# Fused attention and mixture of experts: whole weights eight blocks ahead, conversion beside the first expert, one scatter a block, the end in halves

## The chip, the cores and the metric

The kernel runs on one core of a Trainium2 chip. The metric is device time in microseconds (us) of one execution; three runs of the kernel before gave 1216.66, 1218.28 and 1219.01 us. PE is the matmul engine, DVE, ACT and POOL are the vector, scalar and GpSimd engines, and SP issues the plain DMAs. POOL issues the indirect ones (gathers and scatters by row number).

## The reference

Everything is float32. Three stages follow one another (cut to what is computed):

```python
# 1 attention, 4 batches x 12 heads, 448 tokens, 64 wide
q_n, k_n = rmsnorm(q, g_q), rmsnorm(k, g_k)
attn_out = softmax(q_n @ k_n.T / 8) @ v            # -> x: 1792 tokens x 768
# 2 mixture of experts, 8 experts, each takes exactly 224 tokens
logits = x @ w_gate                                # 1792 x 8
for idx in argsort(-logits.flatten()):             # greedy by rank
    tok, e = idx // 8, idx % 8
    if assigned[tok] < 0 and counts[e] < 224:
        assigned[tok] = e; counts[e] += 1
out[mask_e] = relu(x[mask_e] @ w1[e]) @ w2[e]      # 768 -> 1024 -> 768
# 3 one dense layer over all tokens
h = x @ w_in; g = h * sigmoid(1.702 * h); y = g @ w_out   # 768 -> 2048 -> 768
```

`w_in` and `w_out` are given in 64 bit and are converted to float32 by the kernel itself.

## The kernel before, in words

**Attention** fills the first 330 us: heads are software pipelined in an order written out by hand, and the token rows `x` are written to DRAM (`xd`) pair of heads by pair of heads: `xtok` (transposes into PSUM), `put_x` (scaling by 1/sum on DVE, L305, and a store). For the last three pairs `put_x(pr, True)` copies the PSUM tile on ACT (L301) and scales it on POOL.

**Routing** ranks the tokens for one expert at a time (phase k gives the tokens of expert slot k): `choose`, `row` (PE transposes), compares of every token against every other (`compare`, DVE, L569, L571, and L575 for the diagonal piece `Bd`), rank matmuls (L592, L598), `close` (which expert is full first, a one-hot tile `O` at L643, matmuls at L650, and the row numbers `idx`). Phase 0 (`first`) is done beside the end of attention. After phases 1 and 3 `together` packs the tokens that remain: 16 and 12 scatters on POOL (L695, 112 rows of 40 bytes each, one column `j` of tokens a scatter), then one load of the packed rows `rec` on SP.

**Moe.run** goes through four groups `pr`: expert 2pr, expert 2pr+1, then the dense layer on the 448 tokens of both. An expert is 8 blocks with a tile of `w1` and 6 with a tile of `w2`; the dense part has 16 blocks with a tile of `w_in` (18 matmuls of 448 columns) and 12 with half a tile of `w_out` (24 matmuls). Below, n counts the blocks of an expert or a dense part. Experts 0 and 1 (`FULL`) use the float32 weights as loaded, with 6 or 8 matmuls a block; all others split weights and activations into a high and a low fp32r part (`whi` on ACT, `wlo` on POOL or DVE) and need three matmuls for one. Weights are loaded by `load` into `raw` (4 buffers), at most `LOAD` = 4 blocks ahead of the one in use, in `ahead`.

**Between blocks** `back(budget)` spends a credit: it issues routing steps, each with a cost written in its `yield`, and conversion steps as long as `conv.steps < due`, where `due` grows by `rate` a block. A negative cost ends the routing of that block. As long as phase 1 isn't done only routing is issued. Where a phase is needed at once `until(k)` issues all of its steps: before expert 0, at block 13 of expert 0, at block 5 of experts 2, 4, 6 (for the next expert) and at dense block 20 (for the next pair).

**Conversion** (`Convert`) has 48 pieces of 512 KB: a load, two copies on ACT (`words`, L887 and L888), then two steps, one DVE instruction each (L901, L906), and a 256 KB store. 43 of the 96 steps are issued during attention; `load` of a dense block calls `until(need)` so that its words exist.

**The end**: the last dense block (d = 5) sums 48 matmuls into one tile of 448 columns; then come one copy on ACT (L1115), four transposes (L1120), one copy on DVE (L1125) and four scatters on POOL (L1137).

Of the kernel before, what the change touches and what calls it, by code (L numbers as in the profile page):

```python
# [20 lines left out]
FT = mybir.dt.float32  # L21
# [30 lines left out]
class Attn:  # L52
# [240 lines left out]
            nc.tensor.transpose(p[:, i], s.xuT[pr][:, i * 112:(i + 1) * 112], s.ident128)  # L293
        s.px = p

    def put_x(s, pr, end=False):
        nc, p = s.nc, s.px
        b, pl = divmod(pr, 6)
        if end:
            xt = s.io.tile([112, 4, 256], FT, name="kt", bufs=3)[:, 0:2].rearrange("p a (b c) -> p (a b) c", c=128)  # L300
            nc.scalar.copy(xt, p)  # L301
            p = xt
        else:
            xt = s.wk.tile([112, 4, 128], FT, name="xt", bufs=2)
        (nc.gpsimd if end else nc.vector).tensor_tensor(xt.rearrange("p i (h d) -> p i h d", d=64), p.rearrange("p i (h d) -> p i h d", d=64),  # L305
                                s.rinv[b][:, :, 2 * pl:2 * pl + 2, None].to_broadcast([112, 4, 2, 64]), op=OP.mult)
        nc.sync.dma_start(s.xd[b * 448:(b + 1) * 448, pl * 128:(pl + 1) * 128].rearrange("(i p) d -> p i d", p=112),
                          xt)
# [63 lines left out]
    def run(s, slot, beside):  # L372
# [87 lines left out]
        beside(BESIDE[0])  # L460
        s.gate_b(s.B - 1, 1)
        beside(0)
        for pr in (last - 2, last - 1, last):
            s.xtok(pr, True)
            s.put_x(pr, True)
        beside(BESIDE[1])


class Route:
# [4 lines left out]
    def __init__(s, tc, pool, wk, rec, identf, out_ids, dram):  # L474
# [2 lines left out]
        s.wk, s.rec, s.identf = wk, rec, identf  # L477
        s.L = rec[:, :, 0:8]
        s.done = [None] * 8
        s.pend, s.group, s.moving = [], {}, False  # L480
        ii = wk.tile([112, 224], I32, name="ii", bufs=1)
        s.before = pool.tile([112, 112], FT, name="before")
        nc.gpsimd.iota(ii[:, 0:112], pattern=[[1, 112]], base=0, channel_multiplier=-1)
# [186 lines left out]
    def together(s, n, n2, small):  # L670

        nc, V, wk = s.nc, s.nc.vector, s.wk
        al = s.alive[:, 0:n]
        f = [wk.tile([112, 16], FT, name="f%d" % i)[:, 0:n] for i in range(2)]
        src, sh, i = al, 1, 0
        while sh < n:
            V.tensor_copy(f[i][:, 0:sh], src[:, 0:sh])
            V.tensor_tensor(f[i][:, sh:], src[:, sh:], src[:, 0:n - sh], op=OP.add)
            src, i, sh = f[i], 1 - i, 2 * sh
        V.tensor_tensor(f[i], src, al, op=OP.subtract)  # L680
        yield -1.5
        q = small()[0:112, 0, 0:n]
        nc.tensor.matmul(q, s.before, al, start=True, stop=False)
        nc.tensor.matmul(q, s.ones, f[i], start=False, stop=True)
        yield -0.1
        pos = wk.tile([112, 16], I32, name="pos")[:, 0:n]
        V.tensor_tensor(f[0], q, s.own[:, 0:n], op=OP.subtract)
        V.tensor_tensor(f[0], f[0], al, op=OP.mult)
        V.tensor_tensor(pos, f[0], s.own[:, 0:n], op=OP.add)
        yield -0.5  # L690
        sc = []
        s.moving = True
        for j in range(n):
            nc.gpsimd.memset(s.spacer, 0.0)
            st = nc.gpsimd.indirect_dma_start(  # L695
                out=s.left[n2][:, :], out_offset=bass.IndirectOffsetOnAxis(ap=pos[:, j:j + 1], axis=0),
                in_=s.rec[:, j, :], in_offset=None)
            for x in sc:
                s.tc.declare_no_dep(st.ins, x.ins, reason="rows of other tokens")
            sc.append(st)  # L700
            if j % 2:
                yield -0.05
        s.moving = False
        rec = wk.tile([112, 16, 10], FT, name="rec", bufs=1)[:, 0:n2]
        nc.sync.dma_start(rec, s.left[n2][0:112 * n2, :].rearrange("(p j) c -> p j c", j=n2))
        yield -0.1
        V.tensor_copy(s.ids[:, 0:n2], rec[:, :, 8:10])
        V.memset(s.alive, 1.0)
        s.rec, s.L = rec, rec[:, :, 0:8]
        yield 0.4  # L710
# [33 lines left out]
    def first(s, rank, wide, small, buffer, buffer2):  # L744
# [60 lines left out]
        for j in range(12, 16):  # L805
            compare(j, 12, 16)
        s.flush()
        cnt = wide()
        s.counts(0, 12, cnt)
        nc.scalar.copy(s.ct[:, 12:16], bank[3])  # L810
# [110 lines left out]
class Moe:  # L921
# [15 lines left out]
        s.nl = s.nsp = s.used = 0  # L937
        s.raw, s.hl, s.reg, s.late = {}, {}, {}, {}

    LOAD, SPLIT, LOOK = 4, 2, 5  # L940

    def load(s, n):
        kind, e, i = s.chunks[n]
        if kind in ("w1", "w2") and e not in s.reg:
            s.reg[e] = s.nc.sync.value_load(s.r.eid[0:1, e:e + 1], min_val=0, max_val=7)
        K = 6 if kind == "w1" or (kind == "w32" and i < 16) else 8
        t = s.pw.tile([128, 8, 128], FT, name="raw", bufs=4)[:, 0:K]
        if kind == "w32":
            s.conv.until(s.need(n))
            if i < 16:  # L950
# [33 lines left out]

    def ahead(s):
        N = len(s.chunks)
        while s.nl < N and s.nl < s.used + s.LOAD - (s.used > 0 and s.whole(s.used - 1)):
            kind, e, _ = s.chunks[s.nl]
            if kind != "w32" and not s.r.done[e]:
                break  # L990
            if s.nl >= s.nsp + 4:
                break
            s.load(s.nl)
            s.nl += 1
        while s.nsp < s.nl and s.nsp < s.used + s.SPLIT:
            s.split(s.nsp)
            s.nsp += 1
# [91 lines left out]
    def pair(s, pr, zs):  # L1089
# [12 lines left out]
        s.low()  # L1102
        pend = None
        for d in range(6):
            p = s.ps.tile([128, 448], FT, name="mm", bufs=3)
            for h in range(2):
                w = s.weights()
                for f in range(8):
                    ff = 8 * h + f
                    s.mm3(p, w, f, (gs[:, ff, 0], gs[:, ff, 1]), ff == 0, ff == 15)  # L1110
                if h == 0 and pend:
                    pend()
                yield
            oT = s.pa.tile([128, 448], FT, name="sg", bufs=3)
            nc.scalar.copy(oT, p)  # L1115

            def pend(oT=oT, d=d):
                q = s.ps.tile([112, 4, 128], FT, name="tr", bufs=2)
                for t in range(4):
                    nc.tensor.transpose(q[:, t], oT[:, t * 112:(t + 1) * 112], s.ident128)  # L1120

                def put():
                    if d % 3 == 0:
                        s.ot = s.pa.tile([112, 4, 384], FT, name="ot", bufs=1)
                    nc.vector.tensor_copy(s.ot[:, :, d % 3 * 128:(d % 3 + 1) * 128], q)  # L1125
                    if d % 3 == 2:
                        s.sc += [(pr, s.ot, d // 3, t) for t in range(4)]
                s.ev.append(put)
        s.last = pend

    def store(s, n):
# [30 lines left out]
    def back(s, budget, stay=False, idle=False):  # L1162
# [5 lines left out]
        while s.credit > 0:  # L1168
            if used > 0.5:
                s.low(False)  # L1170
            if not s.r.done[1]:
                c = abs(s.r.step())
            elif s.conv.gen and s.conv.steps < s.due + (0 if route else 2):
                c = s.conv.step()
                if c is None:
                    s.conv.gen = None
# [17 lines left out]
    def run(s):  # L1194
# [6 lines left out]
        s.ahead()  # L1201
        for _ in range(4):
            s.r.step()
        for d in (0, 2, 4):
            s.xsplit(0, d)
            s.r.step()
            s.low()
        for pr in range(4):
            zs = s.pa.tile([128, 6, 2, 448], FR, name="zs", bufs=1)
            for e in (2 * pr, 2 * pr + 1):  # L1210
                early, done = None, 0
                for n, _ in enumerate(s.expert(e, zs)):
# [11 lines left out]
                    if e == 0 and s.r.done[1]:  # L1224
# [3 lines left out]
                        elif n > early + 1 and done < 6:  # L1228
                            s.xsplit(1, done)
                            done += 2  # L1230
                    s.back(0 if n == 7 else (3.1 if e == 0 else 1.4 if e == 1 else 0.6 if n < 8 else 1.2), True if e > 1 and n % 2 == 1 else None, e in IDLE and (e % 2 == 1 or bool(s.r.done[e + 1])))
                if e == 0:
                    s.ahead()
                    for d in range(done, 6, 2):
                        s.xsplit(1, d)
                    s.rate = 0.7
                elif e == 1:
                    s.rate = 1.9
            for n, _ in enumerate(s.pair(pr, zs)):
# [13 lines left out]
def kernel(  # L1253
# [31 lines left out]
    with ExitStack() as actx:  # L1285
# [18 lines left out]

        attn.run(slot, beside)
        for _ in early:
            pass

    rps = ctx.enter_context(tc.tile_pool(name="r_ps", bufs=1, space=bass.MemoryType.PSUM))
    route.start(rps, ctx.enter_context(tc.tile_pool(name="r_wk2", bufs=2)), 1)  # L1310
# [32 lines left out]
```

## Time and profile before

| | |
|---|---|
| runs | 1216.66, 1218.28, 1219.01 us (median 1218.28) |
| the profiled execution's own time | 1219.52 us |
| its span, first to last instruction | 1217.7 us |
| mean granted clock of PE | 0.968 of full |
| busy share of the span | PE 94%, DVE 59%, POOL 53%, ACT 51% |
| data moved | 172.98 MB, mean 142 GB/s |

The profiled execution lies 1.24 us above the median of the runs. The windows further down name a stage by its time: expert 0 375.57 to 425.94, expert 1 to 477.88, the dense part of the first pair to 549.48 (`w_in`) and 616.23 (`w_out`), expert 2 to 653.55, expert 3 to 686.27, and so on. In a view's row "x" is a count, "idle before <-" is the engine's idle time ahead of the instruction and what released it; "remote" is a release that the profile can't put to an instruction.

### The profile page before, as it was taken

To read this page: it belongs to the slowest core of one execution; us is meant where nothing else is said; L and a number is where in the kernel's file an instruction comes from. 1 tells how busy PE (TensorE), PEld (TensorE's weight loads), DVE (VectorE), ACT (ScalarE), POOL (GpSimd) and SP (SyncE) were. 2 spreads that over 40 slices of the span, in tenths; PEclk is the share of its full clock that TensorE was granted. 3 is DMA by queue.
4 is the path that set the end of the run, shared out by engine and by line. 5 is a ranking of instruction groups with operands and counts; after the bars stand their busy time and mean duration, and the time that the engine had idled before them with its cause. 6 is when DMAs were issued, how large, how long until landed. Compare 5 with 4: busy or idle time off the path is not lost.

```text
span 1217.7 us, 20040 instructions
## 1 busy us (share of the span) xinstructions
PE 1146.2 (94%) x7432; PEld 982.7 (81%) x7432; DVE 722.8 (59%) x1398; ACT 626.0 (51%) x1261; POOL 646.6 (53%) x570
## 2 busy tenths in 40 slices
PE   4899999999958979999999999999999999999995
PEld 3677666777536969788899988989998999999994
DVE  7699999999787416989654467454447203421100
ACT  4798889988632124765245544234544324445420
POOL 2688878884430232445555845536444565454552
PEclk9799999999967989999999999999999999999998
DMA  6445464533114657886567534338733345753421
GB/s 160 131 131 144 115 163 127 138 91 89 39 43 125 175 146 214 274 268 223 165 178 192 160 92 133 111 92 211 197 117 116 120 121 166 191 169 107 137 81 34
DMA packets 185505, 172.98 MB, mean 142 GB/s; under 512 B 9536, under 2 KB 159808, under 8 KB 185408
## 3 DMA queue, kind: packets, MB, share of 16 engines
q1 hardware_dynamic: 180080, 160.55, 46.1%
q0 software_dynamic: 4224, 11.14, 3.1%
q8 instruction: 58, 0.95, 0.3%
q14 instruction: 39, 0.32, 0.1%
q10 hardware_dynamic: 1104, 0.03, 0.0%
HBM read 147.96 MB, written 23.72 MB: 141 GB/s over the span
## 4 chain that ended last, share of the span: by engine, by line
PE 78%; DVE 13%; DMA 2%; ACT 2%; issue 2%; POOL 1%; another core or an unknown queue 1%; POOLq 0%; SPq 0%; DVEq 0%; ACTq 0%
PE mm L1042 16%; PE mm L1043 15%; PE mm L1044 15%; PE S L222 7%; PE av L269 6%; PE pA L249 5%; PE mm L1072 3%; DVE wc L901 2%; PE mm L1057 2%; DMA xg<-xd,idx 2%; DVE B L569 2%; PE tp L188 1%; PE tp L203 1%; DVE B L571 1%
## 5 line engine op out<-in xcount | busy, mean ns | idle before, releaser
L978 POOL TENSOR_TENSOR wlo<-raw,whi 128x768 fp32r<-128x768 f32 (+1 forms) x154 | 324.9, 2111 | 354.5 <-ACT whi L975 351.2
L975 ACT CAST whi<-raw 128x768 fp32r<-128x768 f32 (+1 forms) x196 | 182.0, 928 | 137.0 <-issue 44.3
L1042 PE MATMUL mm<-gs,whi 128*128 128x448 f32 (+1 forms) x672 | 224.2, 334 | 0.0
L1043 PE MATMUL mm<-gs,whi 128*128 128x448 f32 (+1 forms) x672 | 220.4, 328 | 0.0
L1044 PE MATMUL mm<-gs,wlo 128*128 128x448 f32 (+1 forms) x672 | 220.3, 328 | 0.0
L1042 PE MATMUL mm<-zs,whi 128*128 128x448 f32 x384 | 144.3, 376 | 0.0
L1044 PE MATMUL mm<-zs,wlo 128*128 128x448 f32 x384 | 141.7, 369 | 0.0
L1043 PE MATMUL mm<-zs,whi 128*128 128x448 f32 x384 | 141.6, 369 | 0.0
L1042 PEld LDWEIGHTS mm<-gs,whi 128*128 128x128 f32 x672 | 128.1, 191 | 7.4 <-issue 1.5
L1044 PEld LDWEIGHTS mm<-gs,wlo 128*128 128x128 f32 x672 | 128.2, 191 | 6.4 <-POOL wlo L978 0.2
L1043 PEld LDWEIGHTS mm<-gs,whi 128*128 128x128 f32 x672 | 128.3, 191 | 5.5
L240 ACT ACTIVATE A<-S,sm 112x448 f32<-112x448 f32 x192 | 122.5, 658 | 6.3 <-DVE sm L233 6.3
L233 DVE TENSOR_REDUCE sm<-S 112x2 f32<-112x896 f32 x96 | 104.1, 1085 | 21.5 <-PE S L222 20.1
L249 PE MATMUL pA<-ident,A 112*112 112x112 f32 x768 | 100.9, 266 | 2.4 <-DVE AT L258 2.3
L249 PEld LDWEIGHTS pA<-ident,A 112*112 112x112 f32 x768 | 85.0, 137 | 14.7 <-DVE AT L258 3.4
L1097 ACT ACTIVATE mm<-mm 128x448 f32<-128x448 f32 x64 | 33.8, 528 | 113.1 <-PE mm L1044 113.1
L222 PE MATMUL S<-khi,qT 128*112 128x448 f32 x192 | 80.7, 420 | 4.5 <-ACT khi L210 4.5
L269 PE MATMUL av<-AT,vt 112*64 112x448 f32 x384 | 82.5, 552 | 0.0
L978 DVE TENSOR_TENSOR wlo<-raw,whi 128x768 fp32r<-128x768 f32 (+1 forms) x42 | 51.2, 1219 | 50.8 <-ACT whi L975 50.8
L1042 PEld LDWEIGHTS mm<-zs,whi 128*128 128x128 f32 x384 | 73.0, 190 | 9.9 <-issue 3.8
L1099 DVE TENSOR_TENSOR gs<-mm,gs 128x448 fp32r<-128x448 f32 x64 | 39.5, 619 | 69.7 <-ACT gs L1098 69.6
L1042 PE MATMUL mm<-xs,whi 128*128 128x224 f32 x288 | 80.0, 278 | 0.9 <-DVE gs L1085 0.9
(222 smaller groups left out, 2405.5 us busy)
## 6 DMA issues: line engine op xcount, KB each, us to landing
raw<-in_moe_w_dram SPq DMA_DIRECT2D x64, 384.0 KB
raw<-in_moe_w_dram SPq DMA_DIRECT2D x48, 512.0 KB
raw<-din SPq DMA_DIRECT2D x64, 384.0 KB
raw<-dout SPq DMA_DIRECT2D x48, 512.0 KB
r<-in_moe_w_in_dram SPq DMA_DIRECT2D x24, 512.0 KB
r<-in_moe_w_out_dram SPq DMA_DIRECT2D x24, 512.0 KB
din<-wc SPq DMA_DIRECT2D x24, 256.0 KB
dout<-wc SPq DMA_DIRECT2D x48, 128.0 KB
```

The source lines that it names most:

```text
L222: nc.tensor.matmul(p[:, c, 0:448], s.qT[h][:, i, :], mv.rearrange("p i t -> p (i t)"), start=(n == 0), stop=(n == 1))
L233: s.nc.vector.tensor_reduce(s.sums[h][:, 2 * u:2 * u + 2, 0], s.Sp[u][:, :, 0:448], axis=AX.X, op=OP.max, negate=True)
L240: s.nc.scalar.activation(s.A[h][:, i, :], p[:, c, 0:448], AF.Exp, bias=sm[:, i, 0:1], scale=1.0, accum_out=sm[:, i, 1:2])
L249: nc.tensor.transpose(p[:, qc], s.A[h][:, qc, kc * 112:(kc + 1) * 112], s.identf)
L269: nc.tensor.matmul(p[hh * 64:(hh + 1) * 64, :], s.grp[g]["v"][:, hl, kc * 64:(kc + 1) * 64], s.AT[h][:, kc, :], start=(kc == 0), stop=(kc ...
L975: nc.scalar.copy(hi, t)
L978: f = lambda: eng.tensor_tensor(lo, t, hi.bitcast(FT), op=OP.subtract)
L1042: nc.tensor.matmul(p, hi[:, k], x[0], start=first, stop=False)
L1043: nc.tensor.matmul(p, hi[:, k], x[1], start=False, stop=False)
L1044: nc.tensor.matmul(p, lo[:, k], x[0], start=False, stop=last)
L1072: nc.tensor.matmul(p, w[:, f], hs[:, f, 0].bitcast(FT), start=f == 0, stop=f == 7)
L1099: s.ev.append(lambda f=f, p=p: nc.vector.tensor_tensor(gs[:, f, 1], p, gs[:, f, 0].bitcast(FT), op=OP.subtract))
```

## The change

1. Weights of experts 0 and 1 are loaded in turn into `raw` (4 buffers), `whi` and `wlo` (3 buffers each, else unused in that stage), up to 8 blocks ahead instead of 4.
2. Conversion steps are issued beside expert 0: 4 ahead of its first block and one a block (14). During expert 1 the rate is 0.8 a block instead of 0.7, with `due` set anew; no conversion runs ahead of its rate by two steps in blocks without routing as long as the rate is at most 1.
3. `together` yields after every scatter, instead of after every second.
4. The last three `put_x` go to DVE like all others, and are issued by `rows` once all compares of phase 0 are.
5. The very last block (pair 3, d = 5) is computed in two halves of 224 columns, each with its own sums, copy, transposes and scatters.

```diff
@@ Attn @@
-    def put_x(s, pr, end=False):
+    def put_x(s, pr):
...
-        if end:
-            xt = s.io.tile([112, 4, 256], FT, name="kt", bufs=3)[:, 0:2].rearrange("p a (b c) -> p (a b) c", c=128)
-            nc.scalar.copy(xt, p)
-            p = xt
-        else:
-            xt = s.wk.tile([112, 4, 128], FT, name="xt", bufs=2)
-        (nc.gpsimd if end else nc.vector).tensor_tensor(xt.rearrange("p i (h d) -> p i h d", d=64), p.rearrange("p i (h d) -> p i h d", d=64),
+        xt = s.wk.tile([112, 4, 128], FT, name="xt", bufs=3)
+        nc.vector.tensor_tensor(xt.rearrange("p i (h d) -> p i h d", d=64), p.rearrange("p i (h d) -> p i h d", d=64),
...
+        s.ends = []
         for pr in (last - 2, last - 1, last):
             s.xtok(pr, True)
-            s.put_x(pr, True)
+            s.ends.append((pr, s.px))
         beside(BESIDE[1])
+
+    def rows(s):
+        for pr, p in s.ends:
+            s.px = p
+            s.put_x(pr)
@@ Route.together @@
-            if j % 2:
-                yield -0.05
+            yield -0.05
@@ Route.first @@
         s.flush()
+        s.ranked = True
+        yield
         cnt = wide()
@@ Moe @@
-    LOAD, SPLIT, LOOK = 4, 2, 5
+    LOAD, SPLIT, DEEP = 4, 2, 8
...
-        t = s.pw.tile([128, 8, 128], FT, name="raw", bufs=4)[:, 0:K]
+        name = ("raw", "whi", "wlo")[n % 3] if s.whole(n) else "raw"
+        if name == "raw":
+            t = s.pw.tile([128, 8, 128], FT, name="raw", bufs=4)[:, 0:K]
+        else:
+            t = s.pw.tile([128, 8, 128], FR, name=name, bufs=3)[:, 0:K].bitcast(FT)
...
-        while s.nl < N and s.nl < s.used + s.LOAD - (s.used > 0 and s.whole(s.used - 1)):
+        while s.nl < N and s.nl < s.used + (s.DEEP if s.whole(s.nl) else
+                                            s.LOAD - (s.used > 0 and s.whole(s.used - 1))):
...
-            if s.nl >= s.nsp + 4:
+            if s.nl >= s.nsp + 4 and not s.whole(s.nl):
                 break
@@ Moe.pair, w_out @@
+            end = pr == 3 and d == 5
+            ws = []
+            for part in ((0, 2), (2, 4)) if end else ((0, 4),):
+                t0, t1 = part
+                x = slice(112 * t0, 112 * t1)
+                p = s.ps.tile([128, 448], FT, name="mm", bufs=3)[:, x]
+                for h in range(2):
+                    if t0 == 0:
+                        ws.append(s.weights())
+                    for f in range(8):
+                        ff = 8 * h + f
+                        s.mm3(p, ws[h], f, (gs[:, ff, 0, x], gs[:, ff, 1, x]), ff == 0, ff == 15)
...
+                nc.scalar.copy(oT, p)
...
+                def pend(oT=oT, d=d, t0=t0, t1=t1):
+                    q = s.ps.tile([112, 4, 128], FT, name="tr", bufs=2)[:, 0:t1 - t0]
+                    for t in range(t1 - t0):
+                        nc.tensor.transpose(q[:, t], oT[:, t * 112:(t + 1) * 112], s.ident128)
...
+                            s.sc += [(pr, s.ot, d // 3, t) for t in range(t0, t1)]
@@ Moe.back @@
-            elif s.conv.gen and s.conv.steps < s.due + (0 if route else 2):
+            elif s.conv.gen and s.rate and s.conv.steps < s.due + (0 if route else 2 if s.rate > 1 else 0):
@@ Moe.run @@
         for _ in range(4):
             s.r.step()
+            s.conv.step()
...
+                    if e == 0:
+                        s.conv.step()
...
-                    s.rate = 0.7
+                    s.due, s.rate = s.conv.steps, 0.8
@@ tile_attention_moe_kernel @@
         for _ in early:
-            pass
+            if route.ranked:
+                attn.rows()
+                route.ranked = False
```

## Rows read from the trace of the kernel before

**Rows 1.** Page: busy us (share of span) and instructions of each engine.

```profile
PE 1146.2 (94%) x7432; PEld 982.7 (81%) x7432; DVE 722.8 (59%) x1398; ACT 626.0 (51%) x1261; POOL 646.6 (53%) x570
```

**Rows 2.** Windows by stage; columns: PE, PEld, DVE, ACT, POOL busy, PEclk, DMA share, GB/s.

```profile
375.57:425.94 50.37, 49.24 (x341) 43.49 (x339) 28.45 (x95) 8.02 (x20) 7.12 (x13) 0.96 0.53 148
425.94:477.88 51.94, 43.41 (x218) 40.23 (x216) 15.21 (x42) 13.55 (x32) 14.96 (x23) 0.90 0.65 185
477.88:549.48 71.60, 69.14 (x382) 60.52 (x375) 66.89 (x117) 48.84 (x82) 33.08 (x17) 0.95 0.83 253
616.23:653.55 37.32, 36.02 (x331) 35.59 (x330) 22.43 (x53) 18.41 (x32) 21.47 (x17) 1.00 0.71 188
856.60:888.76 32.16, 32.16 (x290) 32.16 (x289) 11.61 (x20) 16.54 (x28) 16.13 (x8) 1.00 0.74 206
1142.96:1203.70 60.74, 60.73 (x309) 55.84 (x307) 4.09 (x6) 13.71 (x17) 29.14 (x20) 1.00 0.22 73
```

**Rows 3.** Waits of PE, 425 to 620: total us, times, longest.

```profile
PE mm L1057 <- issue: 4.6, 2, 3.2
PE mm L1057 <- ACT gs L1061: 2.5, 1, 2.5
PE mm L1057 <- DMA raw<-in_moe_w_dram: 1.5, 1, 1.5
PE rc L598 <- DVE Bd L575: 1.4, 1, 1.4
PE rc L650 <- DVE O L643: 1.0, 1, 1.0
```

**Rows 4.** Timeline of ACT in expert 1: start, us, instruction, idle before.

```profile
431.87 0.53 ACT L1032 COPY xs<-tr 128x448 f32<-128x448 f32 x1 [3.23 <-remote]
442.55 0.85 ACT L1061 ACTIVATE gs<-mm 128x224 f32<-128x224 f32 x3 [9.03 <-remote]
```

**Rows 5.** Waits of SP's queue, 425 to 445.

```profile
SPq L958 <- remote: 15.9, 1, 15.9
```

**Rows 6.** Timeline of POOL: first, ninth and last of the 16 scatters of phase 1.

```profile
419.70 0.97 POOL L695 DMA_INDIRECT left<-rec,pos  x1 [4.73 <-DVE pos L689]
...
429.70 1.42 POOL L695 DMA_INDIRECT left<-rec,pos  x1 [0.22 <-issue]
...
439.10 0.94 POOL L695 DMA_INDIRECT left<-rec,pos  x1 [0.22 <-issue]
```

**Rows 7.** Instructions of DVE by line, 360 to 478.

```profile
L901 DVE SCALAR_TENSOR_TENSOR wc<-wab,wc 128x512 int32<-128x512 int32 x5 | 3.4, 687 | 15.4 <-ACT wc L888 12.9 <-issue 2.5
```

**Rows 8.** The same, 478 to 550.

```profile
L901 DVE SCALAR_TENSOR_TENSOR wc<-wab,wc 128x512 int32<-128x512 int32 x16 | 18.1, 1133 | 0.9 <-ACT wc L888 0.9
```

**Rows 9.** The chain that ended last, two gathers: start, us.

```profile
366.51 6.72 DMA xg<-xd,idx
...
834.88 8.20 DMA xg<-xd,idx
```

**Rows 10.** Timeline of DVE: end of phase 0, and a block of compares in expert 0.

```profile
357.75 0.29 DVE L615 TENSOR_SCALAR ra<-tp 112x128 f32<-112x128 f32 x1 [3.27 <-PE tp L606]
...
380.41 2.47 DVE L569 TENSOR_SCALAR B<-vr,v 112x896 f16<-112x896 f32 x4 [5.29 <-PE rc L592]
```

**Rows 11.** Line 305: duration ns min/median/max, first and last start.

```profile
L305 DVE TENSOR_TENSOR xt<-tp,rinv x21: 674/678/692, 63.7 to 311.5; 112x512 f32<-112x512 f32 x21
```

**Rows 12.** Timeline of expert 2, DVE: four one-hot tiles.

```profile
619.35 2.43 DVE L643 TENSOR_SCALAR O<-iota,acc 112x224 f16<-112x224 f16 x4
```

**Rows 13.** Timeline of the end, all engines.

```profile
1203.72 0.53 ACT L1115 COPY sg<-mm 128x448 f32<-128x448 f32 x1 [9.63 <-PE mm L1044]
...
1205.00 0.69 DVE L1125 COPY ot<-tr 112x512 f32<-112x512 f32 x1 [5.44 <-PE tr L1120]
1205.96 0.95 POOL L1137 DMA_INDIRECT out_dram<-ot,idx  x1 [13.77 <-DVE ot L1125]
...
1209.71 0.94 POOL L1137 DMA_INDIRECT out_dram<-ot,idx  x1 [0.22 <-issue]
```

More of the change, by code (lines that the diff above doesn't have):

```diff
@@ L479, in __init__ @@
         s.done = [None] * 8
-        s.pend, s.group, s.moving = [], {}, False
+        s.pend, s.group, s.moving, s.ranked = [], {}, False, False
         ii = wk.tile([112, 224], I32, name="ii", bufs=1)
@@ L1104, in pair @@
         for d in range(6):
[L1105 to L1128, printed above, removed]
+            end = pr == 3 and d == 5
@@ new lines, in pair, with put @@
+            ws = []
[9 more added lines that the diff above has]
+                        s.mm3(p, ws[h], f, (gs[:, ff, 0, x], gs[:, ff, 1, x]), ff == 0, ff == 15)
+                    if h == 0 and pend:
+                        pend()
+                        pend = None
+                    yield
+                oT = s.pa.tile([128, 448], FT, name="sg", bufs=3)[:, x]
+                nc.scalar.copy(oT, p)
[3 more added lines that the diff above has]
+                        nc.tensor.transpose(q[:, t], oT[:, t * 112:(t + 1) * 112], s.ident128)
+                    def put():
+                        if d % 3 == 0:
+                            s.ot = s.pa.tile([112, 4, 384], FT, name="ot", bufs=1)
+                        nc.vector.tensor_copy(s.ot[:, t0:t1, d % 3 * 128:(d % 3 + 1) * 128], q)
+                        if d % 3 == 2:
+                            s.sc += [(pr, s.ot, d // 3, t) for t in range(t0, t1)]
+                    s.ev.append(put)
```

## The prediction

> **What bounds the kernel now.** I read the page first: PE is busy 94% of the span [rows 1], so only what keeps PE waiting, slows its clock or adds instructions to it counts. The windows by stage [rows 2] then say where time above PE's own need lies. A block of a split expert costs PE 32.16 us / 290 instructions = 0.111 us an instruction, with nothing to wait for (expert 5, 856.60), and the last dense part runs at 60.74/309 = 0.197 us: these stages have no slack to give. Three stages have: expert 1 lasts 51.94 us with PE busy 43.41 (8.5 idle) at a mean clock of 0.90; the first `w_in` part 71.60 with 69.14 busy (2.5 idle) at 0.95; expert 2 37.32 with 36.02 busy. With the two levels 2.4 and 1.2 GHz, a mean of 0.90 is up to 0.10 x 51.94 = 5.2 us of clock, 0.95 up to 0.05 x 71.60 = 3.6 us. The list of PE's waits [rows 3] names the idle time: in expert 1 4.6 us "issue", 2.5 for ACT's relu, 1.5 for a weight (`raw`); in the dense part 1.4 for the compare piece `Bd` and 1.0 for the one-hot tile `O`.
>
> The 7.1 us of the first two are one event. In ACT's timeline [rows 4] ACT itself sits 3.23 and then 9.03 us on "remote" until 442.55, a release that the profile can put to no instruction, and SP's queue waits 15.9 us on "remote" for a free buffer [rows 5]. POOL meanwhile issues the 16 scatters of phase 1, from 419.70 to 440.04 [rows 6], one each 1.25 us. I read this as releases held back while the scatters run, not as late data. This decides what part 1 and part 3 can be worth.
>
> **The change part by part.** The terms are against the profiled execution's own 1219.52 us; the median of the runs is 1.24 lower.
>
> *Eight loads ahead, first part.* Before expert 0, eight tiles of 384 KB are asked for instead of four, just as the gather of its rows runs: 366.51 + 6.72 us [rows 9], which is on the chain. Below: 0, if the gather goes beside them. Above: the 6.72 us carried four loads and the rows, 1.57 + 0.69 = 2.26 MB; four loads more at that rate are 4.7 us. The nearest row is the other gather on the chain, 8.20 us beside loads: 1.5 more. I take +1.3 [0, +4.7]. The Trainium skill (DMA: Bandwidth & Descriptors, Queues, rings and completion order) says that an engine goes round its queues packet by packet; by that the gather's queue keeps its turn, the term is 0 and the sum 1.3 lower. No row here shows the four extra loads, and 6.72 against 8.20 doesn't settle it.
>
> *Conversion beside expert 0.* The four steps of the prelude fall into DVE's wait of 5.29 us before 380.41 [rows 10]: 0. Then there is one of 0.687 us [rows 7] a block. A block lasts 50.37/14 = 3.60 us on average and holds 28.45/14 = 2.03 us of DVE [rows 2]; a block of four compares holds 2.47 [rows 10], with the conversion 3.16, still below 3.60. What isn't covered is the last group of compares, to which the pick of the tokens is tied: the eight diagonal ones have a piece `Bd` more, and two to three conversions stand between them: 0.687 x 2.8 = 1.9. Ends: 0, and 14 x 0.687 = 9.6 if each lay on the path. I take +1.9, nearer to the cover that the window shows. ACT's copies for them (14 a stage) fit: ACT is busy 8.02 of 50.37. The transfers: seven pieces of 768 KB in and out are 5.5 MB on 50.37 us, 109 GB/s on top of 148, so 257; the `w_in` part held 253 at a share of 0.83 [rows 2]. It fits, without much to spare.
>
> *Rows of the last pairs.* Three DVE instructions of 0.68 [rows 11], 2.0 us, go into DVE's wait of 3.27 before 357.75 [rows 10], and their stores still end ahead of the gather at 366.5. The three POOL instructions and ACT copies that go were waited for by nobody after the first compares. If the cover were gone it would cost 2.0. 0.
>
> *Expert 1.* With eight loads ahead the 1.45 us for `raw` goes: -1.45. Its other 7.1 us stay: POOL has nothing but scatters in its queue in experts 0 and 1, so a yield after each of them spaces nothing on POOL; it only moves program order, one block a scatter. The load of `rec` (SP) passes from expert 1's block 7 to the first dense part's block 1, and the loads of weights issued up to there no longer stand behind it in SP's queue; phase 2's compares go wholly to the dense part, blocks 4 to 12, its row numbers from block 14 to 20 (at once, by `until`). The rank matmuls that move with them are PE time in either place. Ends: -13.7, all idle and clock of the stage (8.5 + 5.2), and +2, four conversions more in this stage beside scatters, each as the 1.42 against 0.94 us of [rows 6]. The Trainium skill (SBUF — State Buffer, Who interferes with whom) has it that a DVE instruction with two SBUF inputs keeps a GpSimd one that reads SBUF waiting; by that those four add up to 4 x 0.48 = 1.9 us to the scatters, and the sum would be up to 1.9 higher; the row of 1.42 agrees.
>
> *First dense part.* By the counts of the loop's credits, 73 instead of 53 conversion steps are done when it begins, and the rest by block 12 instead of 22. A step costs 1.13 us there [rows 8], against 0.687 earlier: 20 x 1.13 = 22.7 us of 66.89 leave DVE, and six compares come in. The second stall (1.0 for `O`) and its half of the clock loss (1.8) should go, since no conversion is left beside it; the first (1.4) has all of phase 2's compares beside the last conversions now, and stays or grows by 0.8: -2.0. Ends: -6.0 (2.4 + 3.6, all), +3 (the first stall with its clock, 1.4 + 1.8, comes a second time).
>
> *Expert 2.* By the same counts phase 3 is five blocks later, and `until(3)` at block 5 issues three groups of four one-hot tiles at once, where one of them takes up to 2.43 us [rows 12]. Ends: 0 and 3 x 2.43 = 7.3. Most of it goes beside a block's matmuls, and the gather behind it is needed four blocks later: +1.5. The same of expert 4, one group: +0.2 [0, +2.4].
>
> *The end.* 96 matmuls of 224 columns at 0.111 instead of 48 at 0.197: 10.66 - 9.46 = +1.2. The first half's copy, transposes, copy and two scatters lie beside the second half's 5.3 us. Behind the last matmul half-size copies (1205.69 - 1203.72 = 2.0 us before, by estimate 0.8 less), and two scatters less at (1209.71 - 1205.96)/3 = 1.25 [rows 13]: -2.5. Together -2.1 [-2.5, +1.2].
>
> Sum: 1.3 + 1.9 + 0 - 1.45 - 2.0 + 1.5 + 0.2 - 2.1 = -0.65, so 1218.9 for such an execution, and 1217.6 for the median. A measurement of this kernel can tell about 0.2%, 2.4 us, from no change.
>
> **The rivals.** *B, the held releases end.* With ten buffers loaded and none asked for meanwhile, and transfers for the conversion in flight, the 7.1 us and half of the clock loss (2.6) go: 1217.6 - 9.7 = 1207.9. For it: SP's wait of 15.9 us [rows 5] goes with the stall, so that the DMA share is only 0.65, and the first five scatters, still in expert 0, held up nothing: PE is busy 49.24 of its 50.37 us [rows 2, 6]. Against: ACT's relu wants only PE's sums [rows 4], and these don't depend on a load.
>
> *C, slower: transfers in expert 0 don't fit.* 257 GB/s is asked where 253 was the most held. A piece that comes late stops ACT at its copy (L887), the relus and the copies of gathered rows behind it wait, and PE with them after three tiles of sums. A piece of 512 KB at 253 GB/s is 2.1 us late; four of seven: +8.3, 1225.9. It decides once a piece lands after ACT's turn, with two pieces in flight as slack. Against: the pieces are asked for two ahead, some 12 us.
>
> *D, slower: late routing.* Phase 2's and 3's row numbers are both made by `until` now; at the upper end of expert 2's term, 7.3 for 1.5, it is +5.8: 1223.4. It decides when the three groups meet a `wlo` on DVE, as the 2.43 did. That part 3 does nothing on POOL is in the forecast.
>
> **How the numbers follow.** Forecast 0.50, with a range of its own of 1214 to 1222; B 0.25; C 0.15; D 0.10. Bounds at 1215.84 and 1220.7: the forecast gives 0.14 faster, 0.26 same, 0.10 slower; B is faster, C slower, D slower but for 0.01. So faster 0.39, same 0.27, slower 0.34. The range 1207 to 1226 ends at B's and C's times, each with half of its chance outside, and holds the forecast.
>
> **What would show it.** The 16 scatters still 1.25 us apart and ACT still waiting on "remote" some 9 us in expert 1: forecast right, B wrong; no such wait: B. The wait for `raw` gone. Expert 0 near 50.4 + 1.9; over 56 with waits at L887: C. Expert 2 over 42: D. After the last matmul two scatters. Wrong throughout if the time falls by over 12 us: then loads, not scatters, set expert 1.

## The result and the profile after

The changed kernel took 1224.68 us (median of 6 runs, 1221.06 to 1226.53) beside 1217.47 for the kernel before: ratio 1.006, 95% interval 1.0038 to 1.0082. It is 7.2 us (0.6%) slower, where 0.65 us faster was forecast.

Later runs came to other chips, and there the kernel before took 1205 us, or 1215 to 1217. So a time is compared here only with that of the kernel before on its own chip, by the ratio; and stages only between profiles of one kind (below). An unchanged copy of the kernel before once gave 0.9981 (0.9963 to 0.9999) against itself, so a difference of 0.2% is not to be trusted.

The windows of the changed kernel for experts 0 and 1, the first `w_in` part, expert 2 and the last `w_out` part answer to [rows 2] (columns as there):

```profile
377.58:431.57 53.99, 51.95 (x340) 45.15 (x339) 34.88 (x106) 14.13 (x31) 7.31 (x12) 0.92 0.82 231
431.57:475.27 43.70, 38.66 (x194) 37.23 (x193) 10.49 (x19) 15.03 (x33) 14.73 (x23) 0.96 0.75 212
475.27:550.34 75.07, 69.37 (x362) 59.23 (x361) 58.93 (x99) 43.48 (x74) 32.95 (x19) 0.95 0.65 208
617.99:661.22 43.23, 39.95 (x355) 38.87 (x351) 24.41 (x61) 18.75 (x33) 22.06 (x17) 0.96 0.58 170
1150.87:1212.81 61.94, 61.94 (x359) 57.95 (x357) 4.51 (x7) 14.05 (x18) 30.86 (x23) 1.00 0.25 75
```

The profiled execution is 6.0 us longer than that of before (span 1223.7 against 1217.7). In the table a stage lasts from its first matmul to the first of the next stage, and a dense part is taken whole (`w_in` and `w_out`). Beside the first pair stand two profiles of unchanged copies, taken on one other chip; what separates the pairs is told below. All figures are in us, after minus before:

| stage | forecast | first pair | second pair |
|---|---|---|---|
| up to expert 0 | +1.3 | +2.0 | +1.2 |
| expert 0 | +1.9 | +3.6 | +3.9 |
| expert 1 | -1.45 | -8.2 | -1.0 |
| first dense part | -2.0 | +4.4 | +1.2 |
| expert 2 | +1.5 | +5.9 | +5.9 |
| second and third dense part | 0 | +0.7 (-2.5, +3.3) | +0.9 (-2.6, +3.5) |
| experts 4 and 6 | +0.2 | -0.3 | -0.5 |
| the end, from the last `w_out` part | -2.1 | -1.9 | -1.9 |
| whole span | -0.65 | +6.0 | +9.5 |

Four places tell the story. **Ahead of expert 0**, PE's list of waits from 360 to 378 and ACT's timeline:

```profile
PE tr L1036 <- DMA xg<-xd,idx: 5.0, 2, 3.0
PE tr L1036 <- ACT xs L1039: 4.5, 1, 4.5
```

```profile
366.82 0.66 ACT L889 ACTIVATE wab<-r 128x512 f32<-128x512 f32 x1
375.64 0.66 ACT L890 ACTIVATE wc<-r 128x512 int32<-128x512 uint32 x1 [8.16 <-DMA din<-wc]
376.20 0.95 ACT L1039 COPY xs<-tr 128x448 f32<-128x448 f32 x2
```

The second of a conversion's copies (L890) needs one of three `wc` buffers, and waits 8.16 us for the store that empties it. SP issues that store behind all eight loads, and an issue takes SP 0.42 us at the first load and 2.70 at the eighth:

```profile
358.46 0.42 SPq L964 DMA_DIRECT2D raw<-in_moe_w_dram  x1
...
365.43 2.70 SPq L964 DMA_DIRECT2D whi<-in_moe_w_dram  x1
368.23 2.44 SPq L873 DMA_DIRECT2D din<-wc  x1
```

On the chain that ended last it is the step that ends the wait (start, us):

```profile
368.23 7.39 DMA din<-wc
```

The copies of the gathered rows (L1039) stand behind L890 in ACT's queue; PE waits 4.5 us for them. DVE meanwhile shows phase 0 ending 3.4 us earlier than before, 354.31 against 357.75 [rows 10], so the stretch from there to expert 0 is 5.4 us longer. (The next three rows, of later times, are used further down.)

```profile
354.31 0.29 DVE L616 TENSOR_SCALAR ra<-tp 112x128 f32<-112x128 f32 x1 [0.26 <-PE tp L607]
...
490.48 0.18 DVE L707 CAST ids<-rec 112x24 f16<-112x24 f32 x1 [7.01 <-DMA rec<-left]
...
631.38 3.03 DVE L984 TENSOR_TENSOR wlo<-raw,whi 128x768 fp32r<-128x768 f32 x1
634.33 2.33 DVE L644 TENSOR_SCALAR O<-iota,acc 112x224 f16<-112x224 f16 x12
```

**POOL's queue at the end of expert 1** [rows 6 before]: thirteen scatters as before, then each of the last three behind the split of a weight of the dense part. POOL sits 25.23 us ahead of the first split, for ACT's copy `whi` of that weight:

```profile
441.54 0.94 POOL L696 DMA_INDIRECT left<-rec,pos  x1 [0.22 <-issue]
467.72 1.89 POOL L984 TENSOR_TENSOR wlo<-raw,whi 128x768 fp32r<-128x768 f32 x1 [25.23 <-ACT whi L981]
469.55 0.09 POOL L695 MEMSET rspace<- 1x1 f32 x1
469.79 0.95 POOL L696 DMA_INDIRECT left<-rec,pos  x1 [0.15 <-issue]
472.40 1.83 POOL L984 TENSOR_TENSOR wlo<-raw,whi 128x768 fp32r<-128x768 f32 x1 [1.65 <-ACT whi L981]
474.17 0.09 POOL L695 MEMSET rspace<- 1x1 f32 x1
474.41 0.94 POOL L696 DMA_INDIRECT left<-rec,pos  x1 [0.15 <-issue]
476.79 1.94 POOL L984 TENSOR_TENSOR wlo<-raw,whi 128x768 fp32r<-128x768 f32 x1 [1.44 <-ACT whi L981]
478.67 0.09 POOL L695 MEMSET rspace<- 1x1 f32 x1
478.91 1.19 POOL L696 DMA_INDIRECT left<-rec,pos  x1 [0.15 <-issue]
```

So the packed rows come at 490 (DVE's L707 above) instead of 462, as DVE's timeline before has it:

```profile
461.92 0.18 DVE L707 CAST ids<-rec 112x24 f16<-112x24 f32 x1 [13.41 <-DMA rec<-left]
```

The burst of scatters in expert 1 is three scatters shorter, and **expert 2** meets `until(3)` with nothing ready: all twelve one-hot tiles come at once, behind a `wlo` of 3.03 us on DVE (above). The twelve take 2.33 us together, about what the one group of four in [rows 12] took. The hold, as the waits of ACT on "remote" in expert 1 are called below, is still there. From ACT's timeline [rows 4]:

```profile
442.95 0.36 ACT L1068 ACTIVATE gs<-mm 128x224 f32<-128x224 f32 x1 [7.00 <-remote]
```

**The end** is as forecast: POOL has two scatters behind the last matmul instead of four [rows 13].

```profile
1212.13 0.94 POOL L1152 DMA_INDIRECT out_dram<-ot,idx  x1 [0.21 <-issue]
...
1214.47 0.94 POOL L1152 DMA_INDIRECT out_dram<-ot,idx  x1 [1.30 <-DVE ot L1140]
...
1215.71 0.94 POOL L1152 DMA_INDIRECT out_dram<-ot,idx  x1 [0.22 <-issue]
```

### The profile page after: what moved, and what is told of

Read it like the earlier page. It is cut to its first block, busy times and chain, and to the rows that moved or that the text cites. A ratio compares the mean times of both kernels' runs of the same rounds, so it can differ in the third digit from the quotient of the medians.

```text
span 1223.7 us, 20143 instructions
## 1 busy us (share of the span) xinstructions
PE 1147.8 (94%) x7480; PEld 986.4 (81%) x7480; DVE 711.7 (58%) x1402; ACT 624.6 (51%) x1259; POOL 647.3 (53%) x567
## 4 chain that ended last, share of the span: by engine, by line
PE 75%; DVE 14%; DMA 3%; issue 2%; ACT 2%; SPq 1%; POOL 1%; another core or an unknown queue 0%; POOLq 0%; ACTq 0%; DVEq 0%
PE mm L1049 16%; PE mm L1050 15%; PE mm L1051 15%; PE S L222 6%; PE av L269 5%; PE pA L249 5%; PE mm L1079 3%; DVE B L572 2%; PE mm L1064 2%; DVE wc L903 2%; DMA xg<-xd,idx 1%; PE tp L188 1%; DVE sm L233 1%; DVE B L570 1%; PE tp L203 1%
## 5 line engine op out<-in xcount | busy, mean ns | idle before, releaser
L1049 PE MATMUL mm<-gs,whi 128*128 128x448 f32 (+1 forms) x688 | 226.9, 330 | 0.0
L1050 PE MATMUL mm<-gs,whi 128*128 128x448 f32 (+1 forms) x688 | 223.2, 324 | 0.0
L1051 PE MATMUL mm<-gs,wlo 128*128 128x448 f32 (+1 forms) x688 | 223.1, 324 | 0.0
L1049 PEld LDWEIGHTS mm<-gs,whi 128*128 128x128 f32 x688 | 131.2, 191 | 7.1 <-issue 1.4
L1051 PEld LDWEIGHTS mm<-gs,wlo 128*128 128x128 f32 x688 | 131.2, 191 | 6.1 <-POOL wlo L984 0.2
L1050 PEld LDWEIGHTS mm<-gs,whi 128*128 128x128 f32 x688 | 131.2, 191 | 5.3
L1049 PE MATMUL mm<-xs,whi 128*128 128x224 f32 x288 | 81.1, 282 | 3.8 <-DVE gs L1092 2.6
L1050 PE MATMUL mm<-xs,whi 128*128 128x224 f32 x288 | 80.1, 278 | 0.0
```

Of the source, the lines that this page charges most:

```text
L1049: nc.tensor.matmul(p, hi[:, k], x[0], start=first, stop=False)
L1050: nc.tensor.matmul(p, hi[:, k], x[1], start=False, stop=False)
L1051: nc.tensor.matmul(p, lo[:, k], x[0], start=False, stop=last)
```

## The experiments

The theory is that parts 4 and 5 gain some 5 us, that part 3 makes routing late through POOL's queue, and that parts 1 and 2 meet ahead of expert 0. The rivals are that the loads alone do the harm, or the conversions alone. One caution holds for every start of expert 0 below: the end of attention alone (DVE's last copy in L258) lies between 325.5 and 329.2 us in these profiles, and phase 0 and expert 0 move with it.

**Each part alone on the kernel before, one chip.** Parts 4 and 5 (the diff's parts in `put_x`, `rows`, `first` and the `w_out` loop):

> The kernel before with parts 4 and 5 alone (last rows on DVE, last block in halves). Theory: phase 0 ends 3.4 us earlier (its first DVE instruction after the rank sums at 354.3 instead of 357.75) and the end is 2 us shorter, and neither has anything to do with the other parts: about -5.3 us, 1212. Rival, the start is tied to the transfers: the gather of expert 0 is asked for earlier but lands no earlier, only the end's 2 us are left, 1215.5.

The ratio is 0.9914 (0.9884 to 0.9943), in the theory's direction and more than its 5.3 us. In the profile expert 0 starts at 373.12 (2.45 earlier) and the end is 1.9 us shorter. The seven runs scatter widely, from 1204.86 to 1217.22, and the profile is of one of the two slowest (1216.95), so it doesn't show what the fast ones had. The next runs with these parts gave 0.9965, so I take 0.996 for them and leave the rest open.

Part 1 (the first line of its edit; the rest is that of `load` and `ahead` in the change):

```diff
-    LOAD, SPLIT, LOOK = 4, 2, 5
+    LOAD, SPLIT, DEEP = 4, 2, 8
```

> The kernel before with part 1 alone (weights of experts 0 and 1 eight blocks ahead). Theory: with no conversion ahead of expert 0, ACT isn't held there; expert 0 starts at most 1 us later; in expert 1 the 1.45 us wait for a weight goes and the held releases stay: -1.5 to +1 us in all. Rival 1, the eight loads themselves delay the gather: expert 0 starts 4 to 5 us later. Rival 2, loads were what bounded expert 1: it falls from 51.9 to about 44 us, the whole by 7.

The ratio is 0.9988 (0.9966 to 1.0011). Expert 0 starts at 375.87 (+0.3), expert 1 is 1.1 us shorter, and PE's wait for `raw` is gone. This is as the theory has it, and both rivals fall. But phase 0 had ended 2.0 us earlier in this profile (355.76 instead of 357.75), and the gather behind it took 9.01 us instead of 6.72: the loads do delay it, by 2.3 us, half of what the first rival asked.

Part 2 (`s.conv.step()` in the prelude and beside expert 0, and its rates):

> The kernel before with part 2 alone (conversion beside expert 0, and its rate). Theory: ACT is held ahead of expert 0 by a conversion copy that waits for a store queued behind the loads, with four loads about half as long as with eight (4 us instead of 8, +2 us of start); expert 0 grows by 3 to 4 us; the first dense part gains 2 to 3: about +3 us in all, 1220.5. Rival, the conversions are free beside expert 0 and the loss of the whole change is of the scatters alone: -2 to 0 us.

The ratio is 1.0017 (0.9995 to 1.0039). Expert 0 grew by 3.3 us, as the theory has it, but started 2 us earlier, not later (phase 0 had ended 1.8 earlier, at 355.96): behind four loads ACT waits 1.17 us for the store, and PE not at all. The first `w_in` part fell by 5.3 us (the whole dense part by 4.6), and expert 2 grew by 3.0, where PE waits 1.5 us for the gathered rows. From ACT's timeline there:

```profile
370.24 0.67 ACT L888 ACTIVATE wc<-r 128x512 int32<-128x512 uint32 x1 [1.17 <-DMA din<-wc]
```

The theory's figure for the start was wrong, and it stays undecided whether the whole is slower.

Part 3:

```diff
-            if j % 2:
-                yield -0.05
+            yield -0.05
```

> The kernel before with part 3 alone (one scatter a block). Theory: the last three or four scatters of phase 1 come behind weight splits in POOL's queue, some 25 us later, phases 2 and 3 move by five blocks, and expert 2 grows by 5 to 6 us at the forced token numbers; the burst in expert 1 is three scatters shorter, -4 us there; the first dense part +2: about +3 us in all, 1220.5. Rival, late routing costs nothing by itself (it needs the conversions too): -4 to -2 us.

The ratio is 1.0027 (0.9999 to 1.0055), where no change is just inside the interval. Expert 2 is 6.9 us longer, the third dense part 5.0, the first 2.3, and expert 1 is 8.6 us shorter. These are the theory's places, without any conversion beside expert 0; expert 1's gain is twice the 4 us expected.

**Undoing one part of the changed kernel.** Without the prelude's conversions:

```diff
         for _ in range(4):
             s.r.step()
-            s.conv.step()
```

> The changed kernel without the four conversion steps ahead of expert 0. Theory: parts 1 and 2 harm each other there, the copy of a conversion on ACT waits 8.16 us for a store that stands behind eight loads, and the copies of the gathered rows stand behind it in ACT's queue; with the steps gone ACT isn't held, expert 0 starts at 372 to 373 instead of 377.6, and the whole is 4 to 5 us shorter, 1220. Rival, the eight loads delay the gather itself: expert 0 still starts within 1.5 us of 377.6.

In its profile expert 0 starts at 370.12 and PE never waits for `xs`, but attention ended 2.4 us earlier there than in the changed kernel's profile of such a chip, and the profile is of the fastest of four runs. The times don't agree: 1.0095 (1.0064 to 1.0126), no better than the changed kernel on such a chip (1.0093, below). It was run again with the changed kernel beside it:

> The changed kernel, unchanged, as the measure for the next two on the same chip. Theory: 1.006 of before where releases are held in expert 1, 1.009 to 1.012 where not. Rival: neither, the ratio has nothing to do with expert 1.

> The changed kernel without the four conversion steps ahead of expert 0, again. Theory: ACT's wait is on the path to the end; expert 0 starts 5 to 7 us earlier and the time is 4 to 7 us under that of the changed kernel on this chip. Rival: what is won at the start is waited for later (the same conversion steps come later), and the time is within 2 us of it.

The ratios are 1.0060 (1.0035 to 1.0085) and 1.0035 (1.0014 to 1.0055), so 3.3 us lie between the medians, and expert 0 starts at 372.57 instead of 377.04. ACT's copy of the gathered rows waits for no conversion there:

```profile
371.18 0.53 ACT L1039 COPY xs<-tr 128x448 f32<-128x448 f32 x1 [6.38 <-DMA wlo<-in_moe_w_dram]
```

ACT's wait for the store exists and costs PE 4.5 us where it stands. That the whole gets this back is suggested by one pair of runs, with intervals that overlap, and not by the other; it is not shown.

With two scatters a block again:

> The changed kernel with a yield after every second scatter, as before. Theory: the scatters are all out before the weight splits come to POOL, phases 2 and 3 come earlier; expert 2 falls from 43.2 to about 40 us, the first dense part from 142.7 to about 135, the third from 130.9 to 127.7; expert 1 grows by 4 to 5 us as the burst is three scatters longer again: 8 us less in all, 1216.5. Rival, expert 2 and the first dense part are long because of the conversions: both within 1 us of the changed kernel's, and the whole 4 us longer for expert 1.

The ratio is 1.0017 (0.9996 to 1.0038), where the changed kernel gave 1.0093 on another chip on which the kernel before takes 1205 us (below): 0.0076 x 1205 = 9 us. Expert 2 lasts 40.39 us, the first dense part 132.6 and the third 127.8, as the theory has them (the first dense part 2 us shorter still). Expert 1 is 2.2 us longer than the changed kernel's (39.83 against 37.58) and not 4 to 5, as no releases were held on either chip.

Then comes the decisive one: one scatter a block is kept, but the last five of phase 1 go together (of phase 3's twelve, the last two):

```diff
             sc.append(st)
-            yield -0.05
+            if j < 11:
+                yield -0.05
```

> The changed kernel, but the last five scatters of a packing are issued in one block (yields after the first eleven alone), so that all 16 of phase 1 reach POOL's queue ahead of the first weight split. Theory: it is the splits between the last three that make phases 2 and 3 late: the packed rows come some 35 us earlier, the tokens of expert 4 (phase 2's sixth row) before 560 instead of 572, expert 2 lasts 40 to 41 us instead of 43.2, the first dense part 3 to 5 us less: 6 to 10 us less than the changed kernel in all. Rival, one scatter a block costs by program order: the same as the changed kernel within 2 us.

> The changed kernel, unchanged. Theory: where releases are held in expert 1 it is 6 to 7 us slower than before (ratio 1.006, expert 1 8 us shorter); where they aren't, the shorter burst of scatters is worth nothing, expert 1 is as long as before's, and the whole is 12 to 15 us slower, ratio 1.010 to 1.012. Rival: the loss is the same on every chip, 1.006.

The ratio is 1.0019 (1.0000 to 1.0038) against 1.0093 (1.0065 to 1.0120) for the changed kernel on the same chip, which is just under the 1.010 that was expected of it: 9 us for the place of the last scatters. The windows of expert 1, the first `w_in` part and expert 2, first of the changed kernel, then of this one:

```profile
431.54:469.12 37.58, 36.71 (x195) 36.02 (x193) 10.48 (x19) 14.99 (x33) 13.38 (x20) 1.00 0.89 252
469.12:543.05 73.93, 69.32 (x363) 59.30 (x362) 59.03 (x99) 43.48 (x74) 33.67 (x19) 0.95 0.68 213
610.69:653.90 43.21, 39.94 (x355) 38.86 (x351) 24.39 (x61) 18.74 (x33) 22.05 (x17) 0.96 0.58 170
```

```profile
431.98:471.01 39.03, 37.88 (x207) 37.13 (x205) 14.37 (x32) 16.13 (x36) 16.11 (x25) 1.00 0.87 237
471.01:540.92 69.91, 66.01 (x368) 56.51 (x367) 64.42 (x104) 43.50 (x75) 33.47 (x17) 1.00 0.73 224
608.72:648.59 39.87, 37.66 (x333) 37.38 (x332) 22.87 (x53) 18.43 (x32) 22.55 (x17) 0.96 0.65 178
```

The `w_in` part is 4.0 us shorter and expert 2 3.3, while expert 1 is 1.5 longer. The packed rows come 24 us earlier (459.67 instead of 483.34), not the 35 expected. POOL's last scatter now starts before the first split:

```profile
445.69 1.21 POOL L696 DMA_INDIRECT left<-rec,pos  x1 [0.22 <-issue]
462.28 2.37 POOL L985 TENSOR_TENSOR wlo<-raw,whi 128x768 fp32r<-128x768 f32 x1 [15.38 <-ACT whi L982]
```

Both undone, on the chip of after_3:

> The changed kernel without those four steps and with a yield after every second scatter. Theory: the two losses add: 8 to 9 us for the scatters where no releases are held (4 to 5 where they are) and 4 to 7 for the start, 9 to 16 under the changed kernel, ratio to before 0.995 to 0.999. Rival: they don't add, as after a shorter start phase 1 is as late as before: the same as with two scatters alone, 1.002.

The ratio is 1.0021 (0.9998 to 1.0044), so the losses do not add there. Expert 1 lasts 49.3 us instead of 42.2, with the full burst of scatters and ACT waiting 5.34 and 6.78 us on "remote" again. Where releases are held, part 3's shorter burst pays for most of its late routing: against the kernel without the four steps this one gains only 2.1 us between the medians, with overlapping intervals.

**The hold itself.** The kernel before, unchanged, on the chip of after_again:

> The kernel before, unchanged, for a profile of it on the same chip as the three others. Theory: the 12 us between the two chips' times of it are the held releases of expert 1: where ACT has no wait on 'remote' there, expert 1 lasts 39 to 41 us and the kernel about 1206; where it has, 50 to 52 and about 1217. Rival: the chips differ in every stage by a per cent.

The median is 1202.64 us. In the profile (of an execution of 1209.11) expert 1 lasts 38.62 us at full clock, where [rows 2] have 51.94 at 0.90, with the same 16 scatters 1.25 us apart and no wait on "remote":

```profile
426.45:465.07 38.62, 38.52 (x218) 37.32 (x216) 15.20 (x42) 13.65 (x32) 14.99 (x23) 1.00 0.90 250
```

So 13.3 us of expert 1 differ between two profiles of one kernel on two chips. All other stages agree within 2.1 us, a dense part taken whole (in the first, `w_in` is 4.2 us shorter and `w_out` 6.3 longer). I tried to part the scatters:

```diff
+            if n == 16:
+                nc.gpsimd.memset(s.fill, 0.0)
```

> The kernel before with a POOL memset of 112x1024 ahead of each of the 16 scatters of phase 1, so that they don't follow one another at once. Theory: releases are held while POOL issues scatters back to back, and pass in the gaps: no wait of ACT on 'remote' over 2 us in expert 1, which falls by 5 to 8 us; phase 2 comes 15 to 20 us later, which costs expert 2 up to 5: -5 to 0 us in all. Rival, releases are held as long as the packing lasts, whatever stands between the scatters: ACT waits some 15 us longer and expert 1 is 10 us longer.

This run says nothing on the hold, for its chip showed none. The ratio is 1.0074 (1.0043 to 1.0104): with scatters 2.1 us apart phase 2 begins late, and PE, in the middle of expert 1, waits for its first values:

```profile
PE rv L550 <- DVE v L539: 5.6, 1, 5.6
```

**Better than both.** Parts 1, 4 and 5 alone:

> The kernel before with parts 1, 4 and 5 (no conversion beside expert 0, two scatters a block). Theory: the parts don't touch one another; alone, 4 and 5 gave a ratio of 0.9914 and 1 one of 0.9988, so 0.990, about 1205. Rival, the eight loads now meet the earlier gather and take its gain back: 1210 or more, with expert 0 starting after 374.5.

> Parts 1, 4 and 5 again. Theory: 0.996 of before where no releases are held in expert 1, 0.990 where they are (the run of the two parts 4 and 5 alone gave 0.9914 there). Rival: no gain on this chip, 0.999 or more.

The ratios are 0.9964 (0.9946 to 0.9982) on a chip without the hold and 0.9965 (0.9943 to 0.9986) on one with it, some 4 us faster than before on both; the gain where releases are held was not the 0.990 that was expected. Then conversions were added to it, behind the compares only (the line that places them):

```diff
+                    if e == 0 and n >= 7:
+                        s.conv.step()
```

> The kernel before with parts 1, 4 and 5, and with seven conversion steps beside expert 0's blocks 7 to 13 only, behind the compares of phase 1. Theory: ACT and DVE have room there (no compares), so that expert 0 grows by at most 1 us and the first dense part loses 2 to 4: ratio to before 0.990 to 0.994 where no releases are held. Rival, any conversion step there puts DVE behind in the pick of phase 1's tokens: expert 0 +2 to +3, nothing gained over parts 1, 4 and 5 (0.996).

The ratio is 1.0038 (1.0016 to 1.0060), worse than without, and neither account has it. Expert 0 grew by 0.7 us as the theory had it, but expert 1 lasts 45.0 us instead of 38.1 and expert 2 40.6 instead of 37.3. In expert 1 ACT's relus stand behind conversion copies that wait for stores:

```profile
431.63 0.66 ACT L891 ACTIVATE wc<-r 128x512 int32<-128x512 uint32 x1 [3.99 <-DMA dout<-wc]
...
443.62 0.66 ACT L891 ACTIVATE wc<-r 128x512 int32<-128x512 uint32 x1 [5.88 <-DMA dout<-wc]
```

It is the mechanism seen ahead of expert 0, at another place. In expert 2 PE waits 2.1 us for the gathered rows and the clock is 0.96 instead of 1.00.

## Why the prediction was wrong

**The step that failed is part 3**: "POOL has nothing but scatters in its queue in experts 0 and 1, so a yield after each of them spaces nothing on POOL; it only moves program order". From block 12 of expert 1 the dense part's splits are in POOL's queue, and I had counted that the scatters would be issued up to the first dense block, without asking what is queued there by then. The last three wait for splits, the first split for ACT's `whi` until 467.72, and the packed rows come at 490 instead of 462. Putting the last scatters ahead of the splits gave back 9 of the 11 us that the changed kernel loses on that chip (1.0019 against 1.0093). That chip has no hold. Where releases are held, as in the run that was forecast, part 3 alone gave 1.0027 (0.9999 to 1.0055): its late routing is there, but expert 1's shorter burst pays most of it back. So part 3 is the step that was wrong, and not the whole of the 7.2 us.

Against the forecast, the first pair has +6.4 us in the first dense part, +4.4 in expert 2, +1.7 in expert 0 and +0.7 ahead of it, and -6.8 in expert 1. Rival D's 1223.4 lies 1.3 us from the measured time, but its one term is expert 2; that the others nearly cancel is luck.

**Expert 2** was +1.5 of [0, +7.3] and measured +5.9 in both pairs. The place was right (rival D named it, with the `wlo` on DVE), the value was not, and neither was the price of the upper bound: the three groups took 2.33 us together and not 7.3. By the windows 2.0 of the 5.9 us are more idle time of PE (3.3 against 1.3), some 1.7 the clock (0.96 instead of 1.00), and the rest PE's own work, 355 instructions instead of 331. I hid the groups behind a block's matmuls, though they stand behind a `wlo` of 3.03 us, and left out the clock and the matmuls that move there.

**First dense part**: -2.0 was forecast, +4.4 and +1.2 were measured. DVE did lose work (66.89 to 58.93 us busy in the `w_in` part), and alone the conversions were worth -4.6. With part 3 phase 2's compares all start after 490, and PE waits for them: idle time is 5.7 us of 75.07, 3.7 of it for `B` and `v` of the routing, and the clock is 0.95 again. With two scatters a block, where no releases are held, the part lasts 132.6 us instead of before's 140.4. So the gain was there, and larger than -2.0; part 3 spent it.

**Expert 1**: -1.45 was forecast for the weight, and -1.1 measured with part 1 alone, which agrees as far as the hold lets one see (ACT's longest wait on "remote" is 11.1 us there, 9.0 before). The rest of the 8.2 us goes with the shorter burst, again part 3, whose run alone has -8.6. On a chip without the hold expert 1 is 1.0 us shorter, and there PE has 195 instructions instead of 218 in it and hardly waited before (38.52 of 38.62 us busy). Rival B fell: the deeper loads leave the hold.

**Ahead of expert 0**: +1.3 was forecast for the loads in front of the gather. In the seven profiles with the eight loads and without the prelude's conversions the stretch from phase 0's last sums (L615 or its like) to expert 0 is 0.8 to 2.3 us longer than before's 17.8; it is 2.3 with part 1 alone and 0.6 with parts 4 and 5 alone, so the term had about the right size. By the Trainium skill (DMA: Bandwidth & Descriptors, Queues, rings and completion order), as the prediction read it, the term would have been 0; with part 1 alone the gather took 9.01 us instead of 6.72. The prelude's conversions, costed at 0 since DVE waits there, cost 4.5: I looked for cover on DVE, and they were late on ACT, behind a store. It is rival C's mechanism, "stops ACT at its copy", in the prelude instead of expert 0, and with a store's landing instead of a load's.

**Part 4** was "0" and gained 3.4 us: phase 0 ends at 354.31 instead of 357.75. I had filled DVE's wait for PE's sums [rows 10] with the rows, and said that nobody waits for the POOL instructions that go. Nobody does, but DVE's compares run slower beside them. POOL's three scalings before:

```profile
346.14 3.35 POOL L305 TENSOR_TENSOR kt<-kt,rinv 112x512 f32<-112x512 f32 x3 [0.96 <-ACT kt L301]
```

DVE's compares by line, before from 346.3 to 349.6 (beside the scalings) and after from 346.8 to 350.3 (with POOL idle); the last figure ahead of the second bar is the mean in ns:

```profile
L775 DVE TENSOR_SCALAR vt<-vr,v 112x448 f16<-112x448 f32 x3 | 3.6, 1238 | 0.0
L775 DVE TENSOR_SCALAR vt<-vr,v 112x448 f16<-112x448 f32 x10 | 3.7, 441 | 0.0
```

The twelve such compares take 6.8 to 7.0 us in all six profiles that have the scalings on POOL, and 4.4 to 4.6 in the twelve that don't. That is 2.2 of the 3.4 us. The other 1.2 lie between the last compare and L615, where PE's granted clock from 350 to 358 is 0.84 instead of 0.50.

**Expert 0** was forecast at +1.9 and measured at +3.6 and +3.9, alone +3.3. The place was right: PE waits 2.0 us for the last compares instead of 1.1. But that is only 0.9 us; the mean clock is 0.92 instead of 0.96, some 2.3 us, and the clock was no part of the term. **The end** was forecast at -2.1 and measured at -1.9: right, in its parts too (the matmuls +1.2, behind the last matmul -3.1 against -3.3).

## What to carry to other kernels

A yield that spreads instructions of one queue over more blocks places them behind whatever the later blocks put into that queue: list that queue's contents block by block to the last of the moved instructions. A step costed as hidden has to be hidden on every engine and queue that it touches, buffers that are stored from included. An instruction for which nobody waits may still slow another engine beside it, so compare the duration of equal instructions with and without it. Where two edits share a resource, here SP's queue and `wc`, single trials (1.0017 and 0.9988) don't show what they do together.

## What was not expected of the hardware

While thirteen or sixteen scatters some 1.25 us apart run on POOL, ACT waits on "remote" in expert 1, at the longest 3 to 11 us. This is so in nine of the ten profiles from chips on which the kernel before takes 1215 to 1217 us, and in none of the eight from chips on which it takes 1203 to 1205. In all nine the last such wait ends 0.3 to 2.6 us behind the end of the last of these scatters, whether there are thirteen or sixteen. In the tenth profile (after_no_prelude_2) expert 1 is as long as in after_3, 42.2 against 42.1 us, though no wait is put to "remote". That the scatters hold the releases fits all this but was not shown, as the one run that parted them came to a chip without the hold; what differs between the chips stays open too.

DVE's compares of 0.44 us took 1.24 us each beside POOL's scalings, which read and wrote other tiles.
